# An attention and relu-squared kernel on one core: 64-key tiles in quarters of the PE array, transposes of q and k by DMA, one cast-in-DMA load queue, and a fixed place for every piece of attention

## Chip, cores, metric

The kernel runs on one core of one Trainium2 chip. The metric is the device time in microseconds (us); for a single core a run's time is that core's. Before: 474.5 us (median; 474.4 to 475.9).

## The reference

Attention without a softmax (squared ReLU in its place), then a two-layer network with squared ReLU:

```python
# q, k, v: (8 batches, 12 heads, 448 positions, 64), float32; w_in (768, 2048), w_out (2048, 768)
scores = q @ k.T / sqrt(64)
attn   = maximum(scores, 0)**2 / 448
x      = (attn @ v), heads side by side      # (3584, 768)
out    = maximum(x @ w_in, 0)**2 @ w_out     # (3584, 768) float32
```

## The kernel before

Work is cut into 24 units of four heads (three units a batch). For each unit, q and k are loaded as fp32 (SP queue), cast on GpSimd (POOL), transposed on TensorE (PE), scored, squared and multiplied with v (AV below). The two layers (`hps` first, `ops` second; their weights are `w1` and `w2` in the code) run in between as fillers from a queue of steps. Keys are cut as 3 x 128 plus a rest of 64; the rests of two heads share one 128x128 block with zeros beside the diagonal (`kdg`, `vdg`).

```python
def load_diag(dg, src, b, h0, h1):          # 256-byte pieces, POOL queue (casts fp32 to fp16)
    for j in range(2):
        nc.gpsimd.dma_start(out=dg[64*j:64*j+64, h0//2:h1//2, 64*j:64*j+64], in_=src[...KMAIN:S...])
... # loads of q, k; diagonal blocks; v; then all of w1 and w2 at once
def scores(n, hp, t):                        # two heads, 128 keys: two row halves of the array
    sp = s_p.tile([P, 2, 512], FP32, name="sp", tag="s")      # s_p has bufs=2
    for j in range(2):
        r = slice(64 * j, 64 * j + 64)
        nc.tensor.matmul(sp[:, j, 0:S], lhsT=kT[r, hp, t*P:(t+1)*P], rhs=qT[r, hp, :], start=True, stop=True)
... # 16 PE transposes a unit (tq, tk), put singly between other matmuls
def fill(i, ntr):                            # as much layer work as is queued, evenly
    ns = max(0.0, (queued - KEEP) / left)
    ...
```

PSUM holds two score tiles of two banks (`s_p`), two banks for AV or transposes (`av_p`) and two accumulators of one bank (`mm_p`): eight banks in all.

## Time and profile before

| | before |
|---|---|
| time | 474.5 us |
| PE busy | 418.6 us, 88% of the span |
| ACT, DVE busy | 237.9, 215.0 us |
| PE busy in the first 84 us | 40.4 us (sum of the windows) |

First the span in 40 slices of 11.8 us, from the profile's page. A digit is the busy share in tenths; for PEclk it is the clock that was granted to PE, in tenths of full speed.

```profile
PE   1373159999999999999999999999999999999996
...
PEclk9987569999999999999999999999999999999998
DMA  9999999144804283138504382317001210021022
```

PE idles for most of the first six slices, while the DMA engines are full; from slice 7 on it is at 9. Next, two rows of windows. The columns are: window, its length, busy us (instructions) of PE, PE weight load, DVE, ACT, POOL, then granted clock, DMA share and GB/s.

```profile
48.00:60.00 12.00, 2.36 (x15) 1.06 (x15) 0.00 (x0) 1.73 (x2) 7.56 (x15) 0.50 1.19 234
...
192.00:240.00 48.00, 47.11 (x317) 24.14 (x316) 25.50 (x46) 28.50 (x42) 11.30 (x17) 1.00 0.45 95
```

Between 48 and 60 us PE did 2.4 us of work at half clock; from 192 to 240 us 47 of 48. The list of waits (who waited for what: us in total, times, longest) says for what PE stood at the start:

```profile
PE tps L270 <- DMA kdg_95<-in_k_dram: 13.0, 1, 13.0
...
PE tps L270 <- DMA kdg_91<-in_k_dram: 11.3, 1, 11.3
...
PE tps L261 <- POOL qs L99: 6.1, 1, 6.1
```

The small `kdg` loads stood in the queue behind eight weight loads. Last, the timeline of PE at a steady place. Its columns are start, length from the first start to the last end, and what ran; matmuls overlap, so the cost of a group is the distance to the next group's start.

```profile
411.58 0.55 PE L297 MATMUL sp<-qT,kT 64*128 64x448 f16 x4
412.06 1.33 PE L323 MATMUL avt<-at,vs 128*64 128x448 f16 x12
413.32 0.55 PE L329 MATMUL avt<-at,vdg_97 128*128 128x448 f16 x2
413.71 0.81 PE L227 MATMUL ops<-w_0_145,g 128*128 128x384 f16 x4
```

Four score matmuls take 0.48 us to the next start, twelve AV matmuls 1.26: two run at a time (6 x 0.19 = 1.13), and a change between shapes of the array costs about 0.1.

### The profile page before, as it was taken

Reading aid. Unit: us, or ns where it says so; the run is one execution under the profiler, and the core shown is the slowest. Engines: PE = TensorE matmul, PEld = TensorE weight load, DVE = VectorE, ACT = ScalarE, POOL = GpSimd, SP = SyncE. Lnnn points to the kernel's source line nnn. Section 1 sums busy time; section 2 is a strip of 40 time slices with the busy share of each in tenths; the row PEclk is TensorE's granted clock in tenths of the full one; section 3 lists DMA queues with packets and bytes.
Section 4 is the critical chain, followed back from the end, with each engine's and each line's share of the span. In section 5 each row is a group of like instructions: output and inputs, shape, how many; then the busy total and the mean of one; then the engine's idle time right before and its main releaser. Section 6 shows DMA issues by size and latency. Waiting matters only on the chain. (4 is left out here: it accounts for less than half of the span.)

```text
span 473.8 us, 6826 instructions
## 1 busy us (share of the span) xinstructions
PE 418.6 (88%) x2720; PEld 213.0 (45%) x2720; DVE 215.0 (45%) x380; ACT 237.9 (50%) x353; POOL 90.8 (19%) x145
## 2 busy tenths in 40 slices
PE   1373159999999999999999999999999999999996
PEld 0121025455545554545445544555445554555563
DVE  3174045655554336534554346544653445532300
ACT  1183126654655456645654556645663556653421
POOL 6522612124111121313111130313010000000000
PEclk9987569999999999999999999999999999999998
DMA  9999999144804283138504382317001210021022
GB/s 206 239 233 210 230 244 133 37 105 116 148 11 100 87 127 105 40 75 157 114 24 91 105 133 67 79 36 108 19 2 33 68 33 1 1 66 35 0 68 67
DMA packets 58831, 44.48 MB, mean 94 GB/s; under 512 B 27056, under 2 KB 55216, under 8 KB 58800
## 3 DMA queue, kind: packets, MB, share of 16 engines
q1 hardware_dynamic: 28288, 31.46, 23.6%
q0 software_dynamic: 30512, 12.59, 21.7%
q8 instruction: 21, 0.34, 0.3%
q14 instruction: 10, 0.08, 0.1%
HBM read 45.61 MB, written 11.01 MB: 120 GB/s over the span
## 5 line engine op out<-in xcount | busy, mean ns | idle before, releaser
L174 ACT ACTIVATE at<-sp 128x896 f16<-128x896 f32 x168 | 146.1, 915 | 106.3 <-PE sp L297 70.3
L175 DVE TENSOR_TENSOR at<-at 128x896 f16<-128x896 f16 x168 | 105.7, 632 | 137.2 <-ACT at L174 137.2
L227 PEld LDWEIGHTS <-g 128*128 128x128 f16 x896 | 82.1, 98 | 51.7 <-issue 2.1
L174 ACT ACTIVATE g<-hps 128x448 f16<-128x448 f32 x128 | 68.7, 546 | 54.0 <-PE hps L189 53.6
L175 DVE TENSOR_TENSOR g<-g 128x448 f16<-128x448 f16 x128 | 55.2, 436 | 46.0 <-ACT g L174 45.9
L234 ACT ACTIVATE osb<-ops 128x384 f32<-128x384 f32 x56 | 27.5, 491 | 70.8 <-PE ops L227 48.3
L99 POOL CAST qs<-qf 112x512 f16<-112x512 f32 x44 | 30.2, 713 | 143.7 <-issue 141.8
L261 PE MATMUL tps<-ident,qs 112*128 112x112 f16 x192 | 33.0, 224 | 18.0 <-POOL ident masks.py:199 6.2
L227 PE MATMUL ops<-w_0_145,g 128*128 128x384 f16 x224 | 47.2, 326 | 0.8 <-ACT g L174 0.8
L227 PE MATMUL ops<-w_3_151,g 128*128 128x384 f16 x224 | 47.4, 326 | 0.0
L227 PE MATMUL ops<-w_1_147,g 128*128 128x384 f16 x224 | 47.4, 326 | 0.0
L227 PE MATMUL ops<-w_2_149,g 128*128 128x384 f16 x224 | 46.8, 326 | 0.0
L297 PE MATMUL sp<-qT,kT 64*128 64x448 f16 x288 | 42.5, 371 | 4.6 <-DVE kT L278 3.8
L189 PE MATMUL hps<-xt,w_3_143 128*128 128x448 f16 x192 | 42.2, 352 | 0.9 <-ACT g L174 0.9
L189 PE MATMUL hps<-xt,w_0_137 128*128 128x448 f16 x192 | 42.9, 357 | 0.1
L189 PE MATMUL hps<-xt,w_2_141 128*128 128x448 f16 x192 | 41.8, 352 | 0.0
L189 PE MATMUL hps<-xt,w_1_139 128*128 128x448 f16 x192 | 40.4, 352 | 0.3 <-ACT g L174 0.2
L323 PE MATMUL avt<-at,vs 128*64 128x448 f16 x288 | 35.1, 372 | 1.5 <-DMA w_0_137<-in_moe_w_in_dram 1.4
L261 PEld LDWEIGHTS <-qs 112*128 112x128 f16 x192 | 17.7, 102 | 39.8 <-issue 19.0
L99 POOL CAST ks<-kf 128x384 f16<-128x384 f32 x44 | 22.8, 546 | 66.8 <-issue 60.8
L276 DVE COPY qT<-tps 128x896 f16<-128x896 f16 x24 | 14.9, 621 | 35.8 <-PE tps L270 35.7
L270 PE MATMUL tps<-ident,ks 128*128 128x128 f16 x144 | 30.2, 232 | 0.0
(45 smaller groups left out, 244.7 us busy)
## 6 DMA issues: line engine op xcount, KB each, us to landing
qf<-in_q_dram SPq DMA_DIRECT2D x24, 448.0 KB, 4.4
kf<-in_k_dram SPq DMA_DIRECT2D x24, 384.0 KB, 3.6
vs<-in_v_dram POOLq DMA_DIRECT2D x7, 576.0 KB, 6.9
out_dram<-osb SPq DMA_DIRECT2D x8, 336.0 KB, 2.8
out_dram<-osb SPq DMA_DIRECT2D x8, 288.0 KB, 2.6
out_dram<-osb SPq DMA_DIRECT2D x8, 240.0 KB, 2.6
out_dram<-osb SPq DMA_DIRECT2D x8, 192.0 KB, 2.6
out_dram<-osb SPq DMA_DIRECT2D x8, 144.0 KB, 2.5
```

The source lines that it names most:

```text
L99: eng.tensor_copy(dst[:, :, :, j * D:(j + 1) * D], src.rearrange("p (a j) (t d) -> p a j t d", j=2, d=D)[:, :, j])
L174: nc.scalar.activation(out=dst, in_=ps, func=AF.Relu)
L175: nc.vector.tensor_mul(dst, dst, dst)
L189: nc.tensor.matmul(cell[0][:, 0:S], lhsT=w1[f // 4][:, m, (f % 4) * P:(f % 4 + 1) * P], rhs=xt[:, m, :], start=(m == 0), stop=(m == NM - 1))
L227: nc.tensor.matmul(cell[0][:, 0:HALF], lhsT=gt[f][:, tb * P:(tb + 1) * P], rhs=w2[f // 4][:, f % 4, hf * HALF:(hf + 1) * HALF], start=(f = ...
L234: nc.scalar.activation(out=cell[1][:, hf * HALF:(hf + 1) * HALF], in_=cell[0][:, 0:HALF], func=AF.Copy, scale=CO)
L261: nc.tensor.transpose(cell[0][:, 0, o:o + QP], qs[:, hp, j, :], ident[0:QP, 0:QP])
L270: nc.tensor.transpose(cell[0][:, 1, o:o + P], src, ident)
L276: nc.vector.tensor_copy(qT.rearrange("p a c -> p (a c)"), cell[0][:, 0, 0:2 * S])
L297: nc.tensor.matmul(sp[:, j, 0:S], lhsT=kT[r, hp, t * P:(t + 1) * P], rhs=qT[r, hp, :], start=True, stop=True)
L323: nc.tensor.matmul(ap[64 * j:64 * j + 64, hp, 0:S], lhsT=vs[:, 4 * u + 2 * hp + j, t * D:(t + 1) * D], rhs=ats[n, (hp, t)][:, j, :], start ...
```

## The change

Its intent: (1) cut keys as 7 x 64, so that scores and AV use four 64x64 quarters of the array, with no zero blocks; (2) let the DMA engines transpose q and k from unit 6 on, and PE only the first six; (3) load everything early through one casting queue in order of use; (4) merge two key tiles into one activation and one square; (5) give each visit of attention (the scores of two key tiles, and the AV work that is due) a set place in the stream of layer matmuls, and keep every engine in program order. Cut to its core:

```diff
+    ctx.enter_context(tc.manual_schedule())          # engines in program order
-    s_p = ... tc.tile_pool(name="sps", bufs=2, space=PSUM)
+    s_p = ... tc.tile_pool(name="sps", bufs=1, space=PSUM)
+    sps = s_p.tile([P, 4, 512], FP32, name="sps", tag="s")     # ONE tile of four banks
...
+    def load16(n):                                   # units 0 to 5: cast in the DMA, POOL queue
+        nc.gpsimd.dma_start(out=tq, in_=heads(q, n)); nc.gpsimd.dma_start(out=tk, in_=heads(k, n))
+    def load_qk(n):                                  # units 6 on: fp32, SP queue, two buffers
+        nc.sync.dma_start(out=qf, in_=heads(q, n));  nc.sync.dma_start(out=kf, in_=heads(k, n))
+    def dma_transpose(n):
+        nc.sync.dma_start_transpose(out=t, in_=src.rearrange("p j h d -> p (j h d)"))
+    load16(0); load_v(0); load16(1); load_v(1); load16(2); load_v(2); load_w1(0); load_w1(1)
...
+    def pe_transpose(n):
+        for t, src in zip(ts, srcs):                 # q, then k
+            ps = mm_p.tile([P, 1024], FP16, name="tps", tag="mm")     # one of the two accumulators
+            ... 14 transposes ...
+            nc.vector.tensor_copy(t..., ps[:, 0:J * P])
+    def score(t, z):
+        for hh in range(2):                          # rows of the array
+            for hp in range(2):                      # columns
+                nc.tensor.matmul(sps[c, 2*z+hh, 0:S], lhsT=kT[r, j, c], rhs=qT[r, :, c], ...)
+    def soft(tiles, split):                          # batch 0: one activation a tile; later: one for two
+        if split: ... nc.scalar.activation(out=at[:, 2*z:2*z+2], in_=sps[:, 2*z:2*z+2, 0:S], ...)
+        else:     nc.scalar.activation(out=at[:, 0:2*m], in_=sps[:, 0:2*m, 0:S], ...)
+    def enter_unit(n):
+        if n >= 3 and n < NPE: pe_transpose(n)       # NPE = 6
+        m = n + 2
+        if NPE <= m + 1 < NUN: load_qk(m + 1)
+        if NPE <= m < NUN: cast_qk(m); load_v(m); dma_transpose(m)
...
+    events.append((at0 + i * gap, [t, t + 1], t - 3))   # a visit at a set time of the layers' clock
```

## The prediction

> **What bounds it now.** From 96 us to 469 us TensorE bounds the kernel: windows of 48 us show PE busy 47 us, and the chain of waits ends in an almost unbroken run of PE. Before that the loads do: in the first 84 us PE is busy 40 us, at a granted clock of 0.5 to 0.9 (40 slices of the page). The list of waits names 13.0 and 11.3 us for the small `kdg` loads: queued behind eight weight loads, the last landing at about 60 us. Counting cast loads by what they read, 48 to 60 us moved about 373 GB/s, 0 to 30 us about 320.
>
> **PE work, costed from the timeline.** First-layer matmul 0.189 us, second 0.1625: 145 + 146 = 291 us in both kernels. Attention before, per unit of 4 heads: scores 3 x 0.48 + 0.38, AV 1.25 + 0.38, 16 transposes of about 0.05: 4.3 us, 103 us in 24 units. After: 7 score and 7 AV rounds of four 64x64 matmuls. If all four quarters run together a round is 0.19 us; but it needs four 64-column weight loads, which the Trainium skill ("TensorE: Matmul & The Clock Gate", LDWEIGHTS) puts at columns/1.2 = 53 ns, so I estimate 0.215: 3.0 us per unit, 72 us in all. In this trace two halves do run together (12 AV matmuls in 1.25 us); four at once no run shows yet. "TensorEngine Tiling (Array Packing)", Key Properties, says that a change of tiling drains the array; the trace agrees at about 0.1 us (four score matmuls 0.48 instead of 0.38). 66 visits after batch 0: 8 us. Transposes stay on PE for six units only (about 5 us); 18 units go to DMA, off the critical path if they land within two units (25 us).
>
> **Start.** Larger runs (1792 B read), no `kdg`/`vdg`, loads in order of use. At 350 GB/s read: first q and k at 6 to 7 us, unit 2 at 14, the first half of w1 at 24, all six units and weights (20.8 MB) at 63, later with the fp32 loads beside them. Batch 0 becomes bound by ACT: 21 x 0.915 us plus start and flush, ending about 30 us. The first layer of batch 0 with all of batch 1's visits then needs 27 us of PE and of ACT (11 x an estimated 1.66 + 16 x 0.546): about 29 us. I expect one remaining wait near 60 to 72 us: unit 6 needs its DMA transposes, and its v comes behind all of w2: about 5 us.
>
> **Sum.** 30 + 291 + 147 tiles x 2 x 0.215 = 63 + PE transposes 3 + switches 8 + waits about 7 (DMA near 65 us, ACT in the first-layer phases) + tail 4: about 405 us. ACT (about 238 us) and DVE (down to about 175) stay below PE.
>
> **Prediction:** 405 us, 392 to 424. Faster by over 2%: 0.96; within 2%: 0.03; slower: 0.01.
>
> **What would show it.** PE first starts by 7 us; first-layer matmuls start near 30 us; granted clock 1.0 from about 35 us; rounds of four in 0.19 to 0.22 us; merged `at` activations near 1.66 us; PE busy above 95% from 75 us on; transposed q and k waited for by PE in total under 10 us; weights all landed by 75 us.
>
> **What would make it wrong.** Quarters that run only two at a time add 50 us (about 460). Weight loads of 75 ns or more in a row add 25. DMA transposes taking over 10 us each would stall every unit in order. A slower cast-load queue (300 GB/s) adds 10 to 15 us near 65 us.

## The result

The changed kernel takes 432.3 us (431.1 to 434.3), against 474.5. A ratio here is the mean time of one kernel's fast runs over that of the other's fast runs of the same rounds, so it is not quite the ratio of the medians quoted: 0.911 (95% interval 0.908 to 0.914). Executions over 1.5% slower than the fastest of the same kernel are left out of the means. It is faster, as predicted, but by 42 us instead of 70, and outside the range of 392 to 424.

The page after, same rows as before (slices of 10.8 us):

```profile
PE   1665888999999999999999999999999999999995
...
PEclk9995589999999999999999999999999999999998
DMA  9999996554428399725238976734242220001222
```

The start is better filled, but still not full before slice 8, with a granted clock near 0.5 in slices 4 and 5. Two rows of windows:

```profile
12.00:24.00 12.00, 7.84 (x92) 4.20 (x84) 6.07 (x10) 7.18 (x9) 5.43 (x9) 1.00 1.25 205
...
36.00:48.00 12.00, 7.45 (x71) 3.83 (x70) 7.25 (x9) 3.33 (x4) 7.87 (x10) 0.50 1.22 205
```

PE is busy for under 8 of 12 us here. The waits of PE; the only long one left is for the first q:

```profile
PE sps L181 <- ACT at L190: 10.1, 9, 1.8
...
PE tps L164 <- DMA q<-in_q_dram: 7.3, 1, 7.3
...
PE avt L217 <- DVE at L203: 1.9, 1, 1.9
```

The largest sum in the list, 10.1 us, is PE waiting for ACT in nine short pieces. The list doesn't say what they are; the timeline does. First, what a visit of batch 0 looks like (PE scores, then ACT, then PE):

```profile
17.15 0.96 PE L181 MATMUL sps<-qT,kT 64*64 64x448 f16 x8 [0.19 <-ACT at L190]
...
18.16 1.73 ACT L190 ACTIVATE at<-sps 128x896 f16<-128x896 f32 x2 [1.06 <-PE sps L181]
...
19.93 0.96 PE L181 MATMUL sps<-qT,kT 64*64 64x448 f16 x8 [1.08 <-ACT at L190]
```

One visit takes 2.78 us, of which ACT works 1.73: ACT waits 1.06 us for the scores, then PE 1.08 us for ACT. The prediction had ACT working without a gap, 1.83 us a visit. Second, the end of batch 0 and the entry of unit 3:

```profile
40.54 0.94 POOL L109 CAST qs<-qf 128x896 f16<-128x896 f32 x1
41.11 2.37 DVE L203 TENSOR_TENSOR at<-at 128x896 f16<-128x896 f16 x1 [0.98 <-ACT at L190]
...
43.53 0.59 PE L217 MATMUL avt<-at,vt 64*64 64x448 f16 x4 [1.93 <-DVE at L203]
...
44.05 1.30 PE L279 MATMUL hps<-xt,w 128*128 128x448 f16 x3
...
45.28 0.96 PE L164 MATMUL tps<-ident,q 128*64 128x128 f16 x14
...
46.28 0.62 DVE L167 COPY qT<-tps 128x896 f16<-128x896 f16 x1 [1.02 <-PE tps L164]
46.96 0.96 PE L164 MATMUL tps<-ident,k 128*64 128x128 f16 x14 [0.72 <-DVE qT L167]
...
48.63 0.96 PE L181 MATMUL sps<-qT,kT 64*64 64x448 f16 x8 [0.72 <-DVE kT L167]
...
49.53 3.17 PE L279 MATMUL hps<-xt,w 128*128 128x448 f16 x8
```

Between the three first-layer matmuls at 44.05 us and the next ones at 49.53, PE does only unit 3's 28 transposes and its first eight score matmuls, and waits 0.72 us for a copy ahead of k's transposes and again ahead of the scores. The square at 41.11 us (2.37 us long, beside a cast on POOL) had held up the last AV matmuls before that. Third, the steady part, where a visit has two score rounds (x8) and two or three AV rounds (x8, x12):

```profile
205.51 0.57 PE L181 MATMUL sps<-qT,kT 64*64 64x448 f16 x8
...
205.92 0.74 PE L217 MATMUL avt<-at,vt 64*64 64x448 f16 x12
...
206.59 3.01 PE L279 MATMUL hps<-xt,w 128*128 128x448 f16 x15
...
210.18 0.57 PE L181 MATMUL sps<-qT,kT 64*64 64x448 f16 x8
```

From 205.51 to 206.59 us five rounds run: 0.19 us each and 0.13 for changing the array's shape. The whole period, to the next visit at 210.18, is 4.67 us; 15 first-layer and 4 second-layer matmuls account for 3.49 and five rounds for 0.95, which leaves 0.23 us for the two changes of shape. So the quarters do run four at a time. At the very start, the queues' share of the DMA engines in the first 12 us (packets, MB written, share):

```profile
q1 hardware_dynamic: 1088, 1.84, 47.2%
q0 software_dynamic: 1074, 0.91, 46.9%
```

Half of the engines' time went to `q1`, the SP queue. That queue held only the fp32 loads of units 6 and 7, whose first use is a cast at 40.5 us: nothing made SP wait, so it issued all four at 0.7 to 2.3 us, beside the first q and k that POOL issued at 1.2 and 2.1. The first q was used at 7.3 us and the first k at 9.9.

My sum, split at two marks that the trace shows (the split is worked out from the terms of the prediction: 30; then 29 + 24 + about 5 of waits; then the rest), against what came:

| part | predicted | changed kernel | version E7 (below) |
|---|---|---|---|
| to the first first-layer matmul | 30 | 44.1 | 30.1 |
| from there to the first second-layer matmul | 58 | 69.1 | 62.5 |
| from there to the end of the span | 317 | 319.3 | 319.2 |
| sum (span) | 405 | 432.5 | 411.7 |

The steady part is right and the first 88 us are 25 us too short. The experiments are about those.

### The profile page after: what moved, and what is told of

It is laid out like the page before. It is cut to its first block, busy times and chain, and to the rows that moved or that the text cites. A ratio compares the mean times of both kernels' runs of the same rounds, so it can differ in the third digit from the quotient of the medians.

```text
span 432.5 us, 7353 instructions
## 1 busy us (share of the span) xinstructions
PE 398.1 (92%) x3176; PEld 200.8 (46%) x3176; DVE 174.6 (40%) x195; ACT 232.1 (54%) x280; POOL 77.2 (18%) x90
## 3 DMA queue, kind: packets, MB, share of 16 engines
q0 software_dynamic: 15104, 14.55, 21.7%
## 4 chain that ended last, share of the span: by engine, by line
PE 83%; ACT 9%; DVE 3%; DMA 2%; issue 2%; POOL 0%; POOLq 0%
PE ops L315 35%; PE hps L279 30%; PE sps L181 11%; PE avt L217 6%; ACT at L194 5%; ACT at L190 3%; DMA k<-in_k_dram 2%; PE tps L164 1%; ACT g L287 1%; DVE at L203 1%; DVE kT L167 1%; DVE qT L167 0%; DVE g L290 0%; DVE xt L224 0%; POOL q L89 0%
## 5 line engine op out<-in xcount | busy, mean ns | idle before, releaser
L194 ACT ACTIVATE at<-sps 128x1792 f16<-128x1792 f32 (+1 forms) x74 | 122.4, 1654 | 76.8 <-PE sps L181 76.8
L279 PE MATMUL hps<-xt,w 128*128 128x448 f16 x768 | 158.5, 358 | 2.6 <-ACT g L287 2.6
L203 DVE TENSOR_TENSOR at<-at 128x1792 f16<-128x1792 f16 (+1 forms) x95 | 96.3, 1015 | 149.2 <-ACT at L194 137.4
L315 PE MATMUL ops<-w,g 128*128 128x384 f16 x896 | 152.0, 326 | 0.2 <-ACT g L287 0.2
L279 PEld LDWEIGHTS <-w 128*128 128x128 f16 x768 | 72.2, 99 | 84.4 <-issue 24.2
L181 PE MATMUL sps<-qT,kT 64*64 64x448 f16 x672 | 53.1, 391 | 12.7 <-ACT at L190 10.1
L290 DVE TENSOR_TENSOR g<-g 128x896 f16<-128x896 f16 x64 | 48.4, 758 | 33.8 <-ACT g L287 33.2
L217 PE MATMUL avt<-at,vt 64*64 64x448 f16 x672 | 50.5, 376 | 2.2 <-DVE at L203 1.9
L181 PEld LDWEIGHTS <-kT 64*64 64x64 f16 x672 | 14.3, 109 | 44.1 <-issue 39.7
L224 DVE TENSOR_SCALAR xt<-avt 128x896 f16<-128x896 f32 x24 | 26.1, 1087 | 21.2 <-PE avt L217 21.2
L109 POOL CAST ks<-kf 128x896 f16<-128x896 f32 x18 | 22.9, 1272 | 4.8 <-DMA kf<-in_k_dram 4.2
## 6 DMA issues: line engine op xcount, KB each, us to landing
q<-in_q_dram POOLq DMA_DIRECT2D x6, 224.0 KB, 10.8
k<-in_k_dram POOLq DMA_DIRECT2D x6, 224.0 KB, 10.6
```

The costliest lines, as they stand in the source:

```text
L109: nc.gpsimd.tensor_copy(t.rearrange("p j h d -> p h j d"), src.rearrange("p h (j d) -> p h j d", d=D))
L181: nc.tensor.matmul(sps[c, 2 * z + hh, 0:S], lhsT=kT[r, j, c], rhs=qT[r, :, c], start=True, stop=True)
L194: nc.scalar.activation(out=at[:, 0:2 * m], in_=sps[:, 0:2 * m, 0:S], func=AF.Relu, scale=SK)
L203: nc.vector.tensor_mul(at[:, a:a + step], at[:, a:a + step], at[:, a:a + step])
L217: nc.tensor.matmul(ap[64 * hh:64 * hh + 64, hp, 0:S], lhsT=vt[r, hh, j * D:(j + 1) * D], rhs=at[r, hh, :], start=(j == 0), stop=(j == J - 1))
L224: nc.vector.tensor_scalar(out=xts[b][:, 2 * u:2 * u + 2, :], in0=ap[:, :, 0:S], scalar1=CX, scalar2=None, op0=ALU.mult)
```

## The experiments

Theory: four things stretch the start. (a) The single score tile makes scores and activations take turns. (b) The early fp32 loads take bandwidth from the first q and k. (c) The PE transposes at the entry of units 3 to 5 make PE wait for their copies. (d) The half clock that follows from idling makes PE's share of the turns longer. Main rival: the loads bound the start anyway, and mending (a), (c) or (d) only turns into waits for q, k or w1. E1 to E4 ran on one chip, E5 to E8 on a second, E9 and two repeats on a third. The kernel before took 473.9, 474.6 and 474.5 us on them, so medians from different chips can be compared to within about 1 us.

For (a), the compiled program says what the trace hints at. In its list of PE's instructions, the eight matmuls of a visit's two tiles carry one wait on ACT, at the first of the eight, and none at the fifth (line numbers and waits as the program compiles; no run is needed for it):

```
72 L181 Matmult sps<-qT,kT 64x448                        (last of visit 0)
74 L181 Matmult sps<-qT,kT 64x448 [waits Activation_49]  (tile 0 of visit 1)
...
82 L181 Matmult sps<-qT,kT 64x448                        (tile 1 of visit 1)
```

That wait is for the second of the two activations before it. ACT in turn is signalled only by the eighth matmul. So splitting the activation in two, as the change does in batch 0, doesn't help here: the wait covers the whole tile on both sides, and the first score waited for both activations in the loop above (ACT from 18.16 to 19.89 us, scores at 19.93).

**E1, two score tiles in batch 0.**

```diff
-            for z, t in enumerate(tiles): score(t, z)             # halves of sps
+            sp = [sa_p.tile([P, 2, 512], FP32, name="spa", tag="sa") for t in tiles]   # bufs=2, batch 0 only
+            for z, t in enumerate(tiles): score(t, 0, sp[z])
```

> Edit: in batch 0 only, each key tile's scores go to their own 2-bank tile (two of them) instead of halves of the one 4-bank tile. Theory 'serial score tile': a visit of batch 0 falls from 2.4-2.8 us to about 1.9 us (two activations of 0.915), the first-layer matmuls start about 8 us earlier (36 instead of 44 us), and the total falls by 6 to 9 us, to about 424-426. Rival 'loads bound the start': PE then waits for q, k or w1 instead, and the total changes by less than 2 us.

Measured: 421.6 us, ratio 0.889 (0.887 to 0.892); first-layer matmuls from 32.3 us instead of 44.1. In its timeline ACT now runs six activations on end in 5.04 us, and the scores slip in between:

```profile
22.17 5.04 ACT L192 ACTIVATE at<-spa 128x896 f16<-128x896 f32 x6 [0.46 <-PE spa L183]
...
23.14 0.38 PE L183 MATMUL spa<-qT,kT 64*64 64x448 f16 x4 [0.64 <-ACT at L192]
...
23.95 0.38 PE L183 MATMUL spa<-qT,kT 64*64 64x448 f16 x4 [0.43 <-ACT at L192]
```

Theory (a) holds, and the gain of 10.6 us is a little over the expected 6 to 9. The rival is out: PE's waits for DMA stay at 7.3 and 1.6 us, against 7.3 and 1.7 in the changed kernel, all for the first q and k. The gain isn't (a) alone: with PE idling less, the granted clock from 36 to 48 us is 0.92 instead of 0.50.

**E2, the fp32 loads of units 6 and 7 held back.**

```diff
+        if n < NPE + 2:                       # a DVE write in program order, which the load must follow
+            nc.vector.memset(qf[:, 0, 0:1], 0.0); nc.vector.memset(kf[:, 0, 0:1], 0.0)
         nc.sync.dma_start(out=qf, in_=heads(q, n))
```

> Edit: the first two pairs of fp32 q and k loads (units 6 and 7, 1.8 MB), which SP issues at 0.7 us because nothing holds them, get a DVE write of one element of their tile in program order first, so they go out where the program names them. Theory: the first q lands at about 6 us instead of 7.3 and the first k at about 7 instead of 9.9, total -2 to -4 us. Rival (the first loads are slow because of their own queue's start-up): landing times unchanged, total within 1 us.

Measured: 425.5 us, ratio 0.897 (0.894 to 0.900), so 6.7 us instead of 2 to 4. The same view of queues for the first 12 us has one line now:

```profile
q0 software_dynamic: 1857, 1.57, 88.4%
```

The first q was used at 5.1 us and the first k at 6.3. Scores start at 7.9 instead of 11.6 us; first-layer matmuls at 38.1 instead of 44.1. The part that I hadn't expected: the POOL casts of units 6 and 7 also moved, and the last square of batch 0, which took 2.37 us beside a cast in the changed kernel (41.11 us in the fence above), takes 0.62 us here:

```profile
36.94 0.62 DVE L206 TENSOR_TENSOR at<-at 128x896 f16<-128x896 f16 x1 [0.98 <-ACT at L193]
```

That accounts for 1.75 us. Scores start 3.7 us earlier, as expected. Another 2.2 us come later: from the first first-layer to the first second-layer matmul it takes 66.9 us instead of 69.1, with first-layer matmuls at full clock from 42.7 us (eight in 1.69 us; in the changed kernel 3.17 us at 49.5).

**E3, transposes of units 3 to 5 issued ahead.**

```diff
-        if n >= 3 and n < NPE: pe_transpose(n)     # in enter_unit
+        ... pe_transpose(3) after visit 9 of batch 0; 4 and 5 right after the visit one or two before they are needed
```

> Edit: the PE transposes of units 3, 4 and 5 are issued one or two visits before their unit's first score instead of directly before it. Theory 'PE in order waits for the transpose's copies': the gap from the first first-layer matmul to the next run of them (44.1 to 49.5 us) shrinks by 3 to 4 us and units 4 and 5 save about 1.5 us each: total -5 to -8 us. Rival (the time is the transposes' own, wherever they stand): total within 2 us.

Measured: 429.0 us (428.2 without the slow run), ratio 0.903 (0.900 to 0.906): 3 to 4 us, half of what I expected, though more than the rival allows. For unit 3 the theory came true: from the first first-layer matmuls to the next it is now 2.1 us (42.78 to 44.90) instead of 5.5. For units 4 and 5 the place was bad. After a visit, DVE first has to take that visit's square, which waits for ACT; the transposes' copies come behind it and hold both accumulators meanwhile. The waits of E4, which has the same placement, show it (E3's list has the same 2.9 and 2.2, at unit 5 and unit 4):

```profile
PE tps L168 <- DVE qT L171: 2.9, 1, 2.9
PE hps L288 <- DVE qT L171: 2.2, 1, 2.2
```

**E4, all three.**

> All three edits together. If the three causes are separate, the gains add: -14 to -20 us, about 412-418, with first-layer matmuls starting near 33 us and second-layer ones near 95 instead of 113 us. If the loads become the bound, less than 10 us is won and PE waits for w1 or q DMA near 30-45 us.

Measured: 414.7 us, ratio 0.875 (0.873 to 0.876): 17.6 us, against 21.4 for the sum of the three (10.6, 6.7 and, from E3's fast runs, 4.0). The gains nearly add. First-layer matmuls start at 29.8 us, second-layer ones at 93.5 instead of 113.2.

**E6, PE kept busy in batch 0.** Matmuls that nobody reads, only to keep PE from idling.

```diff
         visit(tiles, True, 2 * (i - 2) + 1)
+        dummy(16)                       # 16 matmuls ident x ident into an accumulator
```

> The changed kernel with 16 unused 128x128 matmuls after each visit of batch 0 and 20 at its end, so that PE doesn't idle there; nothing reads them. Theory 'the granted clock of 0.5 between 30 and 56 us costs time': clock stays near 1.0, score groups of eight take 0.57 instead of 0.96 us, first-layer matmuls in the first 10 us of their phase 0.19 instead of 0.38 us: total -5 to -8 us. Rival (the clock is only a sign of idling and costs nothing, because PE waits anyway): within 1.5 us, or slower by the added matmuls.

Measured: 425.5 us, ratio 0.896 (0.894 to 0.898): 6.7 us faster with 196 matmuls more. The window from 36 to 48 us:

```profile
36.00:48.00 12.00, 9.97 (x136) 6.12 (x133) 5.31 (x7) 5.23 (x6) 7.15 (x9) 1.00 1.26 201
```

The granted clock is 1.00 there (0.50 in the changed kernel), first-layer matmuls start at 40.7 instead of 44.1 us, second-layer ones at 104.4 instead of 113.2. A visit of batch 0 falls from 2.78 to 2.40 us, because ACT waits 0.67 us for its scores instead of 1.06:

```profile
20.65 1.73 ACT L190 ACTIVATE at<-sps 128x896 f16<-128x896 f32 x2 [0.67 <-PE sps L181]
```

So (d) is a cost of its own, not a mere sign. But the 6.7 us are not the clock's alone: the last square of batch 0 takes 0.63 us here instead of 2.37, since with everything earlier it no longer runs beside a cast (the first cast starts at 40.8 us), and the added matmuls cost time too. (d) overlaps with the others: in E4 and E7 the mean granted clock is 0.996 without any added matmul.

**E7, transposes just ahead of a visit.** As E4, with `pe_transpose(n)` before the visit instead of behind it.

```diff
-            visit(...);  pe_transpose(n)
+            pe_transpose(n);  visit(...)
```

> As e4_all_three, but the transposes of units 3 to 5 stand just before a visit, so that DVE takes their copies before that visit's square, which has to wait for ACT. In e4 PE stood 2.2 and 2.9 us for these copies behind squares, holding both accumulators. Theory: those two waits go, total 409 to 411 us against 414.6. Rival (the waits move into the first-layer matmuls or onto the loads): within 1.5 us of e4.

Measured: 412.5 us, ratio 0.869 (0.866 to 0.871), 2.2 us under E4 (2.8 by the ratios, which allow for the two chips); I had expected 3.6 to 5.6. Two rows of its page, and PE's waits:

```profile
PE   3779798999999999999999999999999999999995
...
PEclk9999998999999999999999999999999999999999
```

```profile
PE spa L186 <- ACT at L195: 4.1, 9, 0.6
PE hps L288 <- ACT g L296: 2.2, 7, 0.6
PE sps L186 <- DMA kT<-ks: 2.0, 1, 2.0
```

PE waits for a DMA transpose for the first time: 2.0 us at 65 us, for unit 6. This is the wait that the prediction put there at 5 us. The changed kernel and E4 were too late for it to show. So the rival came true in part: at 62.5 us E7 is 4.1 us ahead of E4 (the same run of 14 first-layer matmuls starts at 62.45 and at 66.59), and the wait, with 17 first-layer matmuls at half clock behind it (4.9 us instead of 3.2), takes most of that back.

**E9, unit 6 on PE as well**, to see whether that wait is what is left.

```diff
-    NPE = 6
+    NPE = 7            # and load16(6), load_v(6) ahead of w2
```

> As e7_ahead_of_visit, with unit 6 also loaded as fp16 ahead of w2 and transposed on PE. In e7 PE waits 2.05 us at 65 us for unit 6's DMA transpose of k, and then runs 17 first-layer matmuls in 4.9 instead of 3.2 us at half clock; the transposes on PE cost 1.8 us a unit. Theory (that wait is what is left of the start): the wait goes, second-layer matmuls start about 2 us earlier than 92.5, total 409.5 to 411.5. Rival (the wait moves to unit 7, whose fp32 loads and transposes come later too): within 1 us of e7 or slower.

Measured: 411.9 us, ratio 0.868 (0.867 to 0.870). On the same chip E7 took 412.5 again. The wait is gone, and second-layer matmuls start at 90.5 us, but 0.6 us is no gain that the intervals tell apart. The rival's number came, though not its reason: no wait of PE for a DMA transpose is left in the list, at unit 7 or later. Nothing was lost after 90 us, as the 2 us might suggest: E7's first profile, with second-layer matmuls from 92.5 us, was of its slowest run (413.5 us). On E9's chip E7's profile has them from 91.7 us and a span of 410.9 us; from there to the end it is 319.2 us, in E9 319.4. There E7 waited 2.4 us for the DMA transpose, while E9 reaches the same point 1.2 us later because of unit 6's transposes on PE (14 first-layer matmuls start at 63.59 instead of 62.41). So about half of the wait is paid back.

**E5 and E8, one part undone: all 24 units on PE.** E5 does it in the changed kernel, E8 in E7.

```diff
-    NPE = 6
+    NPE = 24           # fp16 loads for every unit, no casts on POOL, no DMA transposes
```

> The changed kernel with one part undone: all 24 units are loaded as fp16 and transposed on PE at the entry of the unit, as units 3 to 5 are, and no DMA transposes or POOL casts. Theory 'the DMA transposes are worth PE time plus a wait at each unit': 28 transposes cost 0.8 to 1.2 us and the wait for their two copies 1.5 to 2 us (unit 5 stood 2.6 us), for 18 units +35 to +45 us. Rival (only the matmul time counts, as my prediction costed them, 0.8 us a unit): +14 us.

> As e7_ahead_of_visit, with all 24 units transposed on PE and loaded as fp16, no DMA transposes. Theory: once the transposes stand ahead, 18 further units cost only their own PE time, about 0.8 us and a mode switch of 0.1: +14 to +18 us over e7. If it is +35 as in the in-line version, the wait is not a matter of place. If it is under +8, the DMA transposes were worth little.

Measured: E5 469.3 us, ratio 0.991 (0.985 to 0.996); E8 445.1 us, ratio 0.938 (0.936 to 0.941). Without the DMA transposes almost all of the change's gain is gone in E5 (37.0 us of 42). In E8 I was wrong: I expected 14 to 18 us over E7, and it is 32.6. The timeline of a unit in E8 shows why:

```profile
229.24 0.58 PE L165 MATMUL tps<-ident,q 128*64 128x128 f16 x14
...
229.86 0.62 DVE L168 COPY qT<-tps 128x896 f16<-128x896 f16 x1 [1.77 <-PE tps L165]
...
230.54 0.58 PE L165 MATMUL tps<-ident,k 128*64 128x128 f16 x14 [0.72 <-DVE qT L168]
...
231.05 0.57 PE L183 MATMUL sps<-qT,kT 64*64 64x448 f16 x8
```

From 229.24 to 231.05 us a unit costs PE 1.81 us, and 18 x 1.81 = 32.6, about the whole difference (small terms cancel: E8 has 1.9 us more of waits for q and k loads, and lacks E7's 2.0 us for the DMA transpose). The transposes themselves are quick; but PE waits 0.72 us for the copy of q before k's can start. A tile of transposes uses one of two accumulators, and the other one holds an open sum of a layer, so k's tile has to wait until q's is copied. That reading of the two accumulators is argued from the program; what the trace shows is the wait:

```profile
PE tps L165 <- DVE qT L168: 13.4, 18, 1.2
```

It stands 18 times here and 19 times (14.1 us) in E5. Placing the transposes ahead removed only the wait for k's copy (12.6 us in E5). So the DMA transposes (with the loads and casts that go with them, which the two runs undo as well) save more than matmul time: they save the wait for the copy out of PSUM.

**The changed kernel and E7 once more**, on E9's chip.

> The changed kernel unaltered, on the same chip as e9, as a reference for the experiments: ratio 0.911 to before, 431 to 433 us. If it differs by more than 0.5%, the experiments' gains have to be read against this run.

> e7_ahead_of_visit once more on the same chip as e9 and as the changed kernel: 412 to 413 us; its gain over the changed kernel on one chip should be 19 to 20 us.

Measured: 434.2 us (ratio 0.914) and 412.5 us (0.869). The gain of E7 over the change is 21.7 us here (expected 19 to 20) and 19.8 us between the earlier medians; the changed kernel's own runs lie between 431.1 and 435.2 us.

All of them (first-layer and second-layer: start of the first such matmul in the profiled run):

| kernel | median us | ratio to before | first-layer | second-layer |
|---|---|---|---|---|
| changed | 432.3 | 0.911 | 44.1 | 113.2 |
| E1 two score tiles | 421.6 | 0.889 | 32.3 | 101.7 |
| E2 fp32 loads held | 425.5 | 0.897 | 38.1 | 105.1 |
| E3 transposes ahead | 429.0 | 0.903 | 42.8 | 108.5 |
| E4 all three | 414.7 | 0.875 | 29.8 | 93.5 |
| E5 all on PE | 469.3 | 0.991 | | |
| E6 PE kept busy | 425.5 | 0.896 | 40.7 | 104.4 |
| E7 ahead of a visit | 412.5 | 0.869 | 30.1 | 92.5 |
| E8 E7, all on PE | 445.1 | 0.938 | 30.8 | 96.8 |
| E9 E7, seven units on PE | 411.9 | 0.868 | 29.9 | 90.5 |

E7 and E9 beat both kernels, by about 13% and 5%. All runs gave correct results.

## Why the prediction was wrong, point by point

- **Direction and steady part: right.** From the first second-layer matmul to the end I had 317 us, and it took 319.3. Two terms in it were off and cancelled, which was luck. A round of four quarters takes 0.19 us, not 0.215; the weight loads, from which I had estimated 0.215, did not bind. With about 230 rounds (114 tiles scored, a few more multiplied) that is 6 us less. And the changes of shape cost 0.23 us a visit, not 0.12 ("8 us" for 66 visits): with 57 visits 6 us more. I had counted the drain once for each visit, and it is paid going in and coming out.
- **The step that failed, first: "Batch 0 becomes bound by ACT: 21 x 0.915 us plus start and flush, ending about 30 us."** It ended at 44. ACT was not the bound; scores and activations took turns on one PSUM tile, 2.4 to 2.8 us a visit instead of 1.83, and began at 11.6 us because of the next point. The diff showed it (`bufs=1`, one tile of four banks); I trusted the split of the activation to overlap. With two tiles (E1) 10.6 us come back.
- **Second: "At 350 GB/s read: first q and k at 6 to 7 us."** I put the loads in the order of the POOL queue and gave SP's loads their place in the program. SP had nothing to wait for, and issued them at once; k came at 9.9 us. Held back (E2), q and k come at 5.1 and 6.3 us and the kernel gains 6.7.
- **Third: "granted clock 1.0 from about 35 us".** By the clock column it was 0.50 from 31 to 54 us and again from 62 to 64; by the times of the matmuls PE also ran at half speed from its start to about 27 us (eight scores in 0.96 us; the last section comes back to this). Keeping PE busy in batch 0 (E6) gives 6.7 us, up to 1.7 of which is the square.
- **Fourth: "PE transposes 3" us.** Their matmul time was costed, not the waits for their copies: unit 3's took from 45.3 to 48.6 us, unit 5's from 73.4 to 76.0. Moved ahead they give 3 to 4 us (E3), and well placed another 2.2 over E4 (E7).
- **The DMA side: right in kind.** DMA transposes stayed off the critical path, in the changed kernel with no wait at all, and w2 was never waited for. The wait near 65 us exists once the start is mended (2.0 us in E7). What the DMA transposes were worth I had not costed; it is 33 to 37 us (E5, E8).
- **What stays open.** E7 is at 412.5, within the range but 7.5 us over 405. Its start is as predicted (30.1 us). 4.5 us more lie in the two first-layer phases and 2 after them. Waits of 2.2 us for accumulators and 2.0 us for the DMA transpose are seen, and in that profile 1.7 us for the half clock behind the second; the rest was not taken apart. Nor do the single gains of (a) to (d) add up to shares of the 27 us, because they overlap: (d) in particular nearly vanishes when (a) to (c) are mended (mean clock 0.996 in E4). Which of (a) to (c) does that was not separated.

## What to carry to other kernels

When engines run in program order, ask of each tile that two engines share how many of it there are: here one tile, although it was sliced in two, made them take turns, and the list of waits showed that only as short waits. Ask of each queue what holds its first instruction back; here the queue with nothing to wait for ran at once, and took half of the DMA engines' time from what was needed first. And cost a PE transpose with the PSUM tile it holds and the copy it waits for, not with its matmuls alone.

## What the Trainium skill lacked or had wrong

- "TensorE: Matmul & The Clock Gate", LDWEIGHTS: columns/1.2 ns would be 53 ns for a 64-column load. In the trace of the kernel before, such a load took 110 ns (median of 288 for `vs`) and one of 128 columns 98 ns (`w_3_143`); whether these records hold more than the load itself no run shows. The 0.215 us of the prediction is not the page's fault: adding up the four loads of a round was the prediction's own step, and rounds ran every 0.19 us.
- The same page warns in Part 1 that clock events in a trace can be unreliable. Here is a case: in the row from 12 to 24 us the granted clock reads 1.00, while groups of eight score matmuls took 0.96 us as they do later at a clock of 0.50, against 0.57 at full speed.
- The same page, Part 4, gives about 275 ns for one transpose in a kernel's context. The trace shows somewhat less for one alone (median 219 ns in E7; mean 282 in the changed kernel, mostly at half clock), and 14 transposes with 64-partition outputs took 0.43 us from start to start of the next 14 (35.91 to 36.34 us in E7). That part of the page has no figure for a row of transposes.
- "TensorEngine Tiling (Array Packing)", Key Properties, says that a change of mode drains the array, with no figure. Here it is 0.23 us for going into quarters and back.
- "GPSIMD Engine Reference", Specifications, says that POOL shares its SBUF interface with DVE instructions that have two SBUF inputs, with no size there (the skill's page "SBUF — State Buffer" treats the same contention at more length). Here one square took 2.37 us beside a POOL cast instead of 0.62, another in E1 3.43 us at 40.3 us beside two casts instead of 1.09, and the squares of `g` (the second number is the mean in ns) took 758 ns in the changed kernel, and 623 in E8, which has no casts:

```profile
L290 DVE TENSOR_TENSOR g<-g 128x896 f16<-128x896 f16 x64 | 48.4, 758 | 33.8 <-ACT g L287 33.2
```

```profile
L299 DVE TENSOR_TENSOR g<-g 128x896 f16<-128x896 f16 x64 | 39.9, 623 | 36.9 <-ACT g L296 36.1
```
